# Moving element-wise work between VectorE, GpSimd and ScalarE in a fused RWKV-5 attention and mixture-of-experts kernel, and issuing a gather and a flag earlier

## The chip, the core and the metric

The kernel runs on one core of a Trainium2 chip. The metric is the device time of one execution in microseconds. The kernel before was timed three times (378.99 us median, 377.18 to 380.16), and one more execution of it was profiled.

## The reference, cut to what matters

Attention over 4 batches, 8 heads, 768 tokens, head size 48, with a per-channel decay `w` and a bonus `u`; its output, laid side by side over the heads, is the input `x` (4 x 768 tokens, width 384) of a mixture of 8 experts with one expert per token.

```python
for t in range(S):
    kt, vt, rt = (k[:, :, t], v[:, :, t], r[:, :, t])
    cur = np.einsum('bhd,bhe->bhde', u[None] * kt, vt)
    y[:, :, t] = np.einsum('bhd,bhde->bhe', rt, state + cur)
    state = w[None, :, :, None] * state + np.einsum('bhd,bhe->bhde', kt, vt)
...
fresh_e = int(np.argmax(logits[b, s]))
if s == 0 or local_gate[b, s] < 0.5:
    e = fresh_e
else:
    e = prev_e if prev_e >= 0 else fresh_e
...
h = np.maximum(x[b, s] @ w1[e], 0.0)
out[b, s] = p[e] * (h @ w2[e])
```

The kernel has a fast path for decays inside a band and falls back to a general one where a flag says that some decay lies outside, or that an expert has more tokens than its block.

## The kernel before, in words

**Order.** The program is scheduled by hand (`tc.manual_schedule()`): each engine runs its instructions in the order in which the Python emits them, and semaphores join the engines. So the order of the calls in `Attention.run` and `Experts.run` is the order of every queue.

**Attention.** There are 16 items, n = 4 * batch + pair of heads. An item's 768 tokens lie in 6 chunks of 128, and it needs these steps:
- `load` (L189): three transfers on SP, `rk` (r and k, transposed), `kv` and `vT`, three items ahead; four buffers for rk and vT, five for kv.
- `scale` (L203), on GpSimd, called one item ahead: `ke` = k times the decay to the chunk's end (L213), `pd` = r times k (L217), and from item 3 on `rw` = r times the powers of w (`decayed`, L230). Each is two instructions, called halves below; for rw and pd a half is 128 x 384.
- `keys` (L232), on VectorE: `kw` = k times the inverse powers (L237), which lie in PSUM (`inv`). For items 0 to 2 the same function makes rw on VectorE too, from a copy of the powers in PSUM (`first`, part of the PSUM tile `mp`). `reciprocals(i)` (L153) makes the inverse powers of pair i in two VectorE instructions.
- TensorE: `added` (L249) makes the chunks' sums, VectorE's scan in `states` (L255) turns them into states S, `scores` (L291) multiplies kw by rw in two halves of three chunks, VectorE masks each half into `am` (L293), `own` (L268) makes the bonus term, which VectorE multiplies by v (L276), `inside` (L300) adds am times v and `before` (L313) adds S times rw. ScalarE copies the result out of PSUM (L321), `turn` (L332) transposes it, ScalarE copies that into `x` (L334), and after a batch's last pair ScalarE's queue sends x to memory (L337).

Step n of the loop in `Attention.run` holds, in this order: turn(n-2), added(n), states(n), scale(n+1), inside(n-1), before(n-1), the first half of the scores of item n+1 with its mask, the second half of its scores, own(n), keys(n+2), and the mask of the second half. Step 4 makes up the lead: it calls keys for items 4, 5 and 6 and scores for items 4 and 5. The scores, turn and logits share two PSUM tiles (`pairs`), which `banks` hands out by turns: a call waits until the tile of the call before last has been read.

**Routing.** After a batch's last pair, `logits` (L345) and `token_logits` (L351, L352) give the gate logits. Batches 0 and 1 are routed inside the attention's steps 9 to 15: ranks, slots, two one-hot tables (`columns` L813 and `places` L824 on VectorE, `apart`/`same` on ScalarE), `numbers` (L818, GpSimd), and `summed` (L846, TensorE), which turns them into token numbers per expert; `copied` (L852) and `head` (L856, L860, L876, L877) give the indices `gid0`. Then `gather(0)` (L1107) fetches the first expert's 168 token rows from memory with two indirect DMAs on GpSimd's queue.

**Experts.** `Experts.run` holds ten units: two early experts with 168 slots each, filled from batches 0 and 1, then eight blocks. A unit of the first kind runs, for m = 0 to 7, `hidden` (L1134), `output` of m-1 (L1221), then `routing(8 i + m)`, and for the last m the transposes of the next unit's rows (`turn`, L1120, copied out by L1121). `routing(0)` to `routing(12)` route batches 2 and 3 in the same way as above: `routing(4)` emits the ranks, slots and one-hot tables and, last, `blocks` (L783 to L790), all on VectorE; `routing(7)` has `summed`. Expert 0's weights come as four transfers of 768 KB (`piece(0)` to `piece(3)`, L1096, on SP), each behind a one-element copy on ScalarE; expert 1's come on ScalarE's queue at m = 1. All transposes of this part share two PSUM tiles (`tp`), which `bank` hands out by turns.

**The flag.** `flag(0)` (L1693 to L1696, VectorE) counts the decays inside the band on each partition into `some`; `flag(1)` (L1698, TensorE, then L1699 and L1700 on VectorE) adds the partitions up; `flag(2)` joins it with the other count. Parts 0 and 1 are called in `routing(13)` and `routing(14)`, that is at m = 5 and 6 of unit 1.

## Time and profile before

| | us |
|---|---|
| median of three runs | 378.99 (377.18 to 380.16) |
| the profiled execution, its own time | 379.17 |
| its span in the trace | 377.5 |
| attention: until the first `hidden` starts | 113.0 |
| unit 0, until unit 1's first `hidden` starts | 113.0 to 129.4 |
| unit 1, until block 0's first product | 129.4 to 146.1 |
| the eight blocks | 146.1 to 371 |
| TensorE busy | 363.0 (96%) |
| VectorE, GpSimd, ScalarE busy | 247.7, 148.7, 110.3 |
| granted TensorE clock over the span | 0.996 |

A row of the timeline has the start, the time, the engine and line, the operation, output and inputs, shapes and count, and in brackets the idle time of the engine just before it with what ended that. PE is TensorE's stream of matmuls, PEld its loads of weights, DVE VectorE, ACT ScalarE, POOL GpSimd, SP the queue of transfers. Ends of matmuls are modelled, so PE counts as busy while its pipeline drains; the starts of PEld show best when TensorE went on. 96% busy is an average: in the blocks TensorE has no pause, and what can be won or lost lies in the first 146 us.

### The profile page before, as it was taken

How to read it: one execution, taken by the hardware profiler on the slowest of the kernel's cores; microseconds unless marked ns; L12 is line 12 of the kernel's file. 1: busy time of each engine (PE TensorE's matmuls, PEld its weight loads, DVE VectorE, ACT ScalarE, POOL GpSimd, SP SyncE). 2: the span in 40 equal slices, each digit the busy share in tenths (PEclk: the TensorE clock that was granted, in tenths of full speed). 3: DMA queues.
4: the chain of work that ended last, by engine and by line, in shares of the span. 5: the costliest groups of instructions: out<-in, count | busy, mean ns of one | idle time of the engine just before them, and what ended most of it. 6: DMA issues, size and time to landing. Idle time of an engine off the chain costs nothing. (4 is left out here: it accounts for less than half of the span.)

```text
span 377.5 us, 9676 instructions
## 1 busy us (share of the span) xinstructions
PE 363.0 (96%) x3844; PEld 319.6 (85%) x3844; DVE 247.7 (66%) x718; ACT 110.3 (29%) x304; POOL 148.7 (39%) x207
## 2 busy tenths in 40 slices
PE   7899999999989999999999999999999999999992
PEld 6676777786769998999899999999999998989971
DVE  6988778888834835787557656857767767555300
ACT  4132233233532211322332233333243233331210
POOL 7689999786222055212333113313233023021012
PEclk9999999999999999999999999999999999999998
DMA  7999999983669457713352452164165065162011
GB/s 245 417 411 410 407 405 338 370 300 109 196 232 340 160 188 296 299 27 115 140 198 62 147 214 87 49 218 190 38 207 213 22 215 206 21 257 112 2 41 38
DMA packets 17765, 74.93 MB, mean 199 GB/s; under 512 B 2778, under 2 KB 6624, under 8 KB 15408
## 3 DMA queue, kind: packets, MB, share of 16 engines
q1 hardware_dynamic: 10336, 56.89, 40.7%
q0 software_dynamic: 3424, 9.48, 7.4%
q10 hardware_dynamic: 3952, 7.87, 5.7%
q8 instruction: 32, 0.52, 0.6%
q14 instruction: 21, 0.17, 0.1%
HBM read 64.79 MB, written 9.47 MB: 197 GB/s over the span
## 5 line engine op out<-in xcount | busy, mean ns | idle before, releaser
L1333 POOL DMA_INDIRECT out_dram<-yo,sid x27 | 26.6, 985 | 115.5 <-ACT yo L1328 92.0
L1184 PE MATMUL h<-exT,w1t 128*128 128x168 f32 (+4 forms) x240 | 54.9, 327 | 0.0
L1188 DVE TENSOR_TENSOR hT<-h,hs 128x168 f32<-128x168 f32 (+3 forms) x60 | 21.1, 351 | 46.1 <-PE h L1184 29.6
L1107 POOL DMA_INDIRECT xg<-x_d,gid x29 | 31.1, 1072 | 34.1 <-DVE gid L877 15.1
L1184 PEld LDWEIGHTS h<-exT,w1t 128*128 128x128 f32 x240 | 41.6, 190 | 0.3 <-issue 0.3
L1134 PE MATMUL h<-exT,w1t 128*128 128x168 f32 (+2 forms) x192 | 37.2, 333 | 0.5 <-DVE lt L698 0.5
L1253 PE MATMUL y<-factors,sums 128*128 128x192 f32 x168 | 36.8, 326 | 0.0
L293 DVE TENSOR_TENSOR am<-pair,kept 128x768 f32<-128x768 f32 x32 | 30.0, 953 | 8.9 <-PE pair L291 8.4
L217 POOL TENSOR_TENSOR pd<-rk 128x384 f32<-128x384 f32 x32 | 31.5, 1006 | 10.6 <-PE y L268 10.0
L1184 PE MATMUL h<-xs,ws 128*128 128x168 f32 (+4 forms) x144 | 35.3, 327 | 0.0
L1134 PEld LDWEIGHTS h<-exT,w1t 128*128 128x128 f32 x192 | 30.9, 190 | 2.6 <-DVE lt L698 0.6
L1184 PEld LDWEIGHTS h<-xs,ws 128*128 128x128 f32 x144 | 25.5, 190 | 4.3 <-ACT hs L1191 1.2
L1253 PEld LDWEIGHTS y<-factors,sums 128*128 128x128 f32 x168 | 28.9, 190 | 0.2
L291 PE MATMUL pair<-rw,kw 48*64 48x128 f32 (+1 forms) x768 | 23.4, 249 | 1.9 <-issue 1.1
L300 PE MATMUL y<-am,kv 128*64 128x128 f32 x360 | 22.9, 276 | 1.3 <-DVE y L276 1.2
L230 POOL TENSOR_TENSOR rw<-rk,tab 128x384 f32<-128x384 f32 x26 | 23.7, 936 | 0.4 <-DMA rk<-in_rk_dram 0.4
L1121 DVE COPY exT<-tp 128x384 f32<-128x384 f32 (+5 forms) x29 | 13.9, 485 | 14.7 <-PE tp L1120 14.6
L291 PEld LDWEIGHTS pair<-rw,kw 48*64 48x64 f32 x768 | 19.6, 133 | 4.6 <-issue 2.8
L1253 PE MATMUL y<-w2t,hT 128*128 128x192 f32 x96 | 23.0, 328 | 0.0
L213 POOL TENSOR_TENSOR ke<-kv,endT 128x288 f32<-128x288 f32 (+1 forms) x32 | 21.9, 705 | 1.9 <-DMA kv<-in_kv_dram 1.0
L321 ACT COPY xT<-y 128x768 f32<-128x768 f32 x15 | 12.0, 800 | 33.1 <-PE y L313 31.1
L300 PEld LDWEIGHTS y<-am,kv 128*64 128x64 f32 x360 | 19.4, 137 | 2.4 <-DVE y L276 1.7
(298 smaller groups left out, 736.6 us busy)
## 6 DMA issues: line engine op xcount, KB each, us to landing
w1t<-in_w_dram SPq DMA_DIRECT2D x8, 1536.0 KB, 6.9
w2t<-in_w_dram SPq DMA_DIRECT2D x8, 1536.0 KB
rk<-in_rk_dram SPq DMA_DIRECT2D x15, 768.0 KB, 8.4
kv<-in_kv_dram SPq DMA_DIRECT2D x16, 584.0 KB, 7.1
vT<-in_vT_dram SPq DMA_DIRECT2D x16, 384.0 KB
x_d<-x ACTq DMA_DIRECT2D x4, 1152.0 KB
w1t<-in_w_dram SPq DMA_DIRECT2D x2, 768.0 KB
w2t<-in_w_dram SPq DMA_DIRECT2D x2, 768.0 KB
```

The source lines that it names most:

```text
L213: nc.gpsimd.tensor_mul(t["ke"][:, z], t["k"][:, z], spread(self.endT[:, p, hp], 1, len(range(NCH)[z])))
L217: nc.gpsimd.tensor_mul(t["pd"][:, z], t["rT"][:, z], t["kT"][:, z])
L230: engine.tensor_mul(t["rw"][:, z], t["rT"][:, z], spread(pw, 1, z.stop - z.start))
L291: nc.tensor.matmul(sc[f * DP:(f + 1) * DP, h, i, x:], lhsT=t["kw"][q, c, o * DP:(o + 1) * DP], rhs=t["rw"][q, c, x:], start=True, stop=True)
L293: return lambda: nc.vector.tensor_mul(t["am"][:, g], sc, spread(self.kept[:, g:g + 3], 1, 2))
L300: nc.tensor.matmul(t["y"][h][p * DP:(p + 1) * DP, c2 * P:(c2 + 1) * P], lhsT=t["v"][:, (2 * c + h) * DH:(2 * c + h) * DH + DP], rhs=t["am" ...
L1107: self.nc.gpsimd.indirect_dma_start(out=xg[:n], out_offset=None, in_=self.x_d[:rows], in_offset=bass.IndirectOffsetOnAxis(ap=u["gid"][:n, ...
L1134: nc.tensor.matmul(h[:, :n], lhsT=u["w1"][:, m, kk, :], rhs=u["xT"][:, kk, :], start=(kk == 0), stop=(kk == DK - 1))
L1184: nc.tensor.matmul(out, lhsT=a, rhs=b, start=start and k == 0, stop=stop and k == len(terms) - 1, skip_group_check=True)
L1188: nc.vector.tensor_tensor(out, a, b, op=Alu.add)
L1253: return lambda: nc.tensor.matmul(bank[:, x * half:(x + 1) * half], lhsT=a, rhs=b, start=(j == 0 and x == 0), stop=(j == FK // 2 - 1), ski ...
L1333: self.nc.gpsimd.indirect_dma_start(out=out.rearrange("n (h d) -> (n h) d", h=2) if half else out, out_offset=bass.IndirectOffsetOnAxis(ap ...
```

## The change

It does the following.
- **Start.** `reciprocals(1)` on VectorE becomes `inverse(1)`: three GpSimd instructions of 128 x 128 and a ScalarE copy into PSUM. Three warming transposes go. Item 2's second half of rw goes from VectorE to GpSimd, ahead of pd.
- **Items 3 to 8** (`SHARED`). The second half of rw goes from GpSimd to VectorE, right behind kw, read from the table in SBUF.
- **Items 14 and 15** (`LATE`). kw goes from VectorE to GpSimd, ahead of pd, from a copy (`held`) of the inverse powers that ScalarE makes in step 8.
- **Routing of batches 0 and 1.** `columns` moves ahead of the last mask of step 13, `places` is cut in two (end of step 13, middle of step 14), `same` moves to the start of step 14, `numbers` ahead of pd(15), and `summed` and `copied` to the end of step 14, with added(15) ahead of them. `head` and the two gathers move to the start of step 15. The number tables (`numbering`, `cast`) move from steps 2 and 6 to step 8.
- **Transfers.** kv of item 4 is issued ahead of its rk. `piece(1)` stays at the end of the attention's step 14, `piece(3)` is issued behind the gathers, and waits for their rows by a one-element copy on GpSimd.
- **Last item.** `before(15)` runs chunk by chunk over both heads, as for other items, instead of head by head. `own(15)` is no longer cut by `summed`.
- **First unit.** The transposes of unit 0's rows come right after logits(3), ahead of `token_logits` and of `turn(15)`; the second tile's copy goes to ScalarE. So does one of the four copies for block 0.
- **Flag.** `flag(0)` and `flag(1)` move from `routing(13)` and `routing(14)` to `routing(5)` and `routing(6)`; the matmul of `flag(1)` gets its weights spread over 128 columns.

The diff, cut to its core:

```diff
@@ -51,6 +51,8 @@
+LATE = (B * HP - 2, B * HP - 1)
+SHARED = range(3, 9)
@@ -156,6 +159,14 @@
+    def inverse(self, i):
+        nc, w, inv = self.nc, self.tab[:, i, 0, 1:], self.tab[:, i, 1, 1:]
+        nc.gpsimd.tensor_mul(self.more, w, inv)
+        nc.gpsimd.tensor_scalar(self.more, self.more, -1.0, 2.0, Alu.mult, Alu.add)
+        nc.gpsimd.tensor_mul(self.more, self.more, inv)
+        nc.scalar.copy(self.inv[:, i], self.more)
@@ -190,22 +201,25 @@
+        if n == AHEAD:
+            nc.sync.dma_start(out=kv, in_=self.kv_d[b, hp])
...
-        nc.sync.dma_start(out=kv, in_=self.kv_d[b, hp])
+        if n != AHEAD:
+            nc.sync.dma_start(out=kv, in_=self.kv_d[b, hp])
...
-    def scale(self, n):
+    def scale(self, n, ahead=None):
@@ -217,26 +231,44 @@
         def rw(i):
-            self.decayed(nc.gpsimd, n, slice(i * C2, (i + 1) * C2))
+            if i == 0 or n not in SHARED:
+                self.decayed(nc.gpsimd, n, slice(i * C2, (i + 1) * C2))
+        if n == 2:
+            rw(1)
         for what in (pd, ke) if n < 3 else (ke, rw, pd) if n == 4 else (rw, ke, pd):
+            if n in LATE and what is pd:
+                self.keys(n, nc.gpsimd)
+                if ahead:
+                    ahead()
             for i in range(2):
                 what(i)
...
-        pw = self.first[:, :P] if n < 3 else self.tab[:, t["hp"], 0, :P]
+        pw = self.first[:, :P] if n < 3 and engine is self.nc.vector else self.tab[:, t["hp"], 0, :P]
...
-    def keys(self, n):
+    def keys(self, n, engine=None):
+        if n in LATE and not engine:
+            return
         nc, t = self.nc, self.items[n]
+        engine = engine or nc.vector
         t["kw"] = self.two.tile([P, NCH, P], F32, name="kw")
-        inv = self.inv[:, t["hp"]]
-        for z in (slice(0, NCH),) if n > 2 else (slice(0, C2), slice(C2, NCH)):
-            nc.vector.tensor_mul(t["kw"][:, z], t["kT"][:, z], spread(inv, 1, z.stop - z.start))
-            if n < 3:
+        self.room(n)
+        inv = self.held[:, n - LATE[0]] if n in LATE else self.inv[:, t["hp"]]
+        for z in (slice(0, NCH),) if 2 < n < LATE[0] else (slice(0, C2), slice(C2, NCH)):
+            engine.tensor_mul(t["kw"][:, z], t["kT"][:, z], spread(inv, 1, z.stop - z.start))
+            if n < 2 or n == 2 and z.start == 0:
                 self.decayed(nc.vector, n, z)
+        if n in SHARED:
+            self.decayed(nc.vector, n, slice(C2, NCH))
@@ -307,7 +336,7 @@
-        for c, h in [(c, h) for h in range(2) for c in range(1, NCH)] if last else [(c, h) for c in range(1, NCH) for h in range(2)]:
+        for c, h in [(c, h) for c in range(1, NCH) for h in range(2)]:
@@ -376,9 +405,8 @@
                 self.turn_ends(slice(1, HP))
-                self.warm(3)
+                self.inverse(1)
                 self.added(0)
-                self.reciprocals(1)
@@ -398,12 +426,15 @@
                     self.reciprocals(2)
-                else:
-                    router.numbering()
...
                 self.turn(n - 2, pair("tp"))
+                if n == g + 6:
+                    router.same(0, 1)
+                if n == g + 7:
+                    router.head(self.pairs[0][:, 1, C2 * P:])
+                    heads()
@@ -411,7 +442,7 @@
-                    if n not in (g + 3, g + 5):
+                    if n not in (g + 3, g + 5, g + 7):
...
                         self.states(n)
@@ -425,10 +456,10 @@
+            if n == HP * 2:
+                router.numbering()
             if n + 1 < M:
-                self.scale(n + 1)
-            if n == g + 6:
-                router.numbers(0, self.nc.gpsimd)
+                self.scale(n + 1, (lambda: router.numbers(0, self.nc.gpsimd)) if n == g + 6 else None)
@@ -436,12 +467,12 @@
-            if n == g + 6:
-                router.same(0, 1)
-            if M - 2 <= n < M:
-                fetch(2 * (n - M + 2) + 1)
-            if n == 6:
+            if n == M - 2:
+                fetch(1)
+            if n == HP * 2:
                 router.cast()
+                self.held = self.late.tile([P, len(LATE), P], F32, name="held")
+                self.nc.scalar.copy(self.held, self.inv[:, HP - len(LATE):])
@@ -449,14 +480,9 @@
             if n == g + 7:
-                self.own(n, 0)
-                router.summed(0, 0)
-                self.own(n, 1)
-                router.copied(0)
+                self.own(n)
                 spare = self.py.tile([P, 2, 512], F32, name="y")
                 self.turn(n - 1, [spare[:, 0], spare[:, 1]])
-                router.head(self.pairs[0][:, 1])
-                heads()
@@ -465,6 +491,8 @@
                 self.scores(ahead, 0)()
+                if n == g + 6:
+                    router.places(0, slice(3, 6))
                 keep = self.scores(ahead, 1)
@@ -494,6 +522,8 @@
                     self.keys(n + 2)
+                if n == g + 5:
+                    router.columns(0)
                 if 3 < n and ahead < M:
                     keep()
@@ -501,10 +531,12 @@
             if n == g + 5:
-                router.columns(0)
                 router.apart(0, 1)
+                router.places(0, slice(0, 3))
             if n == g + 6:
-                router.places(0, 0)
+                self.added(n + 1)
+                router.summed(0, 0)
+                router.copied(0)
@@ -1092,7 +1123,10 @@
         src = (self.w2 if w else self.w1)[u["e"]].rearrange("p (m x) -> p m x", m=FK)
-        nc.scalar.copy(t[0:1, z.start, 0:1], self.ident[0:1, 0:1])
+        if k == 3:
+            nc.gpsimd.tensor_copy(t[0:1, z.start, 0:1], u["xg"][-1][0:1, 0:1])
+        else:
+            nc.scalar.copy(t[0:1, z.start, 0:1], self.ident[0:1, 0:1])
@@ -1110,7 +1144,7 @@
-    def turn(self, i, j):
+    def turn(self, i, j, copy=None):
@@ -1118,7 +1152,7 @@
-        nc.vector.tensor_copy(u["xT"][:, :, j * P:j * P + n], tp[:, :, :n])
+        (copy or nc.vector.tensor_copy)(u["xT"][:, :, j * P:j * P + n], tp[:, :, :n])
@@ -1403,10 +1437,13 @@
             r.numbers(1)
-            r.places(1, 0)
-            r.places(1, 1)
+            r.places(1, slice(0, 6))
+            r.places(1, slice(6, 12))
             r.blocks()
+        if s == 5:
+            self.flag(0)
         if s == 6:
+            self.flag(1, bank("fp"))
             self.fetch(EARLY, self.nc.sync, 1)
@@ -1428,10 +1465,6 @@
-        if s == 13:
-            self.flag(0)
-        if s == 14:
-            self.flag(1, bank("fp"))
@@ -1441,10 +1474,10 @@
         yb = [self.yps.tile([P, 512], F32, name=f"y{d}") for d in range(DK)]
         att.logits(B - 1, yb[0])
+        for j in range(len(self.units[0]["rows"])):
+            self.turn(0, j, self.nc.scalar.copy if j else None)
+        att.token_logits(B - 1, yb[0])
         att.turn(B * HP - 1, yb[1:])
-        self.turn(0, 0)
-        att.token_logits(B - 1, yb[0])
-        self.turn(0, 1)
         self.router.powers(0)
@@ -1566,7 +1599,7 @@
-                    self.turn(i + 1, m - (FK - after))
+                    self.turn(i + 1, m - (FK - after), self.nc.scalar.copy if following and m == FK - 3 else None)
@@ -1680,7 +1713,7 @@
-        att.run(router, ex.piece, lambda: ex.gather(0))
+        att.run(router, ex.piece, lambda: (ex.gather(0), ex.piece(3)))
@@ -1695,7 +1728,7 @@
-                nc.tensor.matmul(fp[:1, :1], lhsT=some, rhs=router.ones[:, 0:1], start=True, stop=True)
+                nc.tensor.matmul(fp[:, :1], lhsT=some.to_broadcast([P, P]), rhs=router.ones[:, 0:1], start=True, stop=True)
```

23 lines of the change are left out of this document (12 added, 11 removed).

## The prediction

> **What bounds the kernel now.** The page's slices put TensorE at 96% with the clock at full, so I asked first for the busy time by stretches.
>
> ```profile
> 10.00:20.00 10.00, 8.95 (x191) 7.08 (x191) 9.11 (x17) 1.71 (x3) 7.04 (x9) 1.00 1.02 411
> ...
> 30.00:40.00 10.00, 9.05 (x199) 6.31 (x198) 8.16 (x11) 2.11 (x5) 10.00 (x13) 1.00 1.02 408
> 40.00:50.00 10.00, 9.94 (x245) 8.20 (x244) 7.14 (x28) 3.22 (x11) 9.93 (x12) 1.00 1.03 408
> ...
> 110.00:120.00 10.00, 8.94 (x64) 8.19 (x64) 4.33 (x22) 3.00 (x10) 2.46 (x4) 1.00 0.71 249
> ...
> 140.00:150.00 10.00, 9.31 (x63) 8.64 (x61) 6.12 (x21) 2.24 (x7) 5.51 (x10) 1.00 0.68 253
> ```
>
> Columns: TensorE, weight loads, VectorE, ScalarE, GpSimd, clock, DMA. TensorE has pauses in four places only: the first 40 us, the end of the attention, and one spot near 143. From 40 us on it is full although GpSimd is as full as it was before: GpSimd has run ahead and is not what TensorE waits for. So taking work off GpSimd in items 3 to 8 can win nothing there, and work added to VectorE can only cost. Past 146 us TensorE is full to the end; what it loses earlier is never given back. The rest of the reading is the timeline at these places.
>
> **Start.** VectorE sets the pace of steps 1 and 2:
>
> ```profile
> 8.93 1.56 POOL L213 TENSOR_TENSOR ke<-kv,endT 128x288 f32<-128x288 f32 x2
> ...
> 10.89 1.97 POOL L217 TENSOR_TENSOR pd<-rk 128x384 f32<-128x384 f32 x2 [0.40 <-DMA rk<-in_rk_dram]
> ...
> 12.22 0.30 DVE L156 SCALAR_TENSOR_TENSOR mp<-mp,tab 128x128 f32<-128x128 f32 x1 [0.63 <-PE mp L249]
> ...
> 13.32 0.53 DVE L237 TENSOR_TENSOR kw<-rk,inv 128x384 f32<-128x384 f32 x1
> ...
> 14.70 0.55 DVE L230 TENSOR_TENSOR rw<-rk,mp 128x384 f32<-128x384 f32 x1
> ...
> 15.30 0.54 PEld L291 LDWEIGHTS pair<-rw,kw 48*64 48x64 f32 x24 [0.30 <-DVE rw L230]
> ...
> 18.12 1.53 PE L300 MATMUL y<-am,kv 128*64 128x128 f32 x24 [0.82 <-DVE y L276]
> ```
>
> `inverse(1)` takes two instructions of 0.30 us off VectorE. With the three warming transposes gone as well, added(0) and the scan behind it come some 0.5 us earlier, and kw(1) starts near 12.4 instead of 13.32. The new path must be in time. No row shows a 128 x 128 multiplication on GpSimd; by ke (0.78 us for 288 columns) three of them take 1.0 us, with bounds of 0.7 and 1.6. From 10.49, where ke ends, that gives 11.5, and the ScalarE copy 11.9, so it is hidden behind added(0) and the scan by 0.5 us; at the upper bound it is late by 0.1. pd(1) moves from 10.89 to 11.5 and ends by 13.5, before own(1). In step 2 the half of rw that leaves VectorE frees 0.46 us (the spacing of these instructions); on GpSimd it fits in ahead of pd(2). I carry 0.9 plus what step 2 adds to its masks, **1.1 us won**; bounds 0 (the transfers of items 1 and 2, which the row of 10.89 shows late by 0.40, take its place) and 1.6. kv(4) ahead of rk(4) in SP's queue only swaps two transfers that are used near 27 us. The number tables leave GpSimd near 20 us, where it next waits for a transfer: nothing; in step 8 they lie beside its waits for own.
>
> **Items 3 to 8.** In steps 5 and 6 the mask of the second half of the scores frees the PSUM tile that the next scores need:
>
> ```profile
> L230 POOL TENSOR_TENSOR rw<-rk,tab 128x384 f32<-128x384 f32 x26 | 23.7, 936 | 0.4 <-DMA rk<-in_rk_dram 0.4
> ```
> ```profile
> 34.66 1.82 DVE L293 TENSOR_TENSOR am<-pair,kept 128x768 f32<-128x768 f32 x2 [1.17 <-PE pair L291]
> ...
> 45.43 1.97 POOL L217 TENSOR_TENSOR pd<-rk 128x384 f32<-128x384 f32 x2
> ...
> 46.26 0.94 DVE L237 TENSOR_TENSOR kw<-rk,inv 128x768 f32<-128x768 f32 x1
> ...
> 47.12 0.95 DVE L293 TENSOR_TENSOR am<-pair,kept 128x768 f32<-128x768 f32 x1
> ...
> 48.33 0.14 PEld L291 LDWEIGHTS pair<-rw,kw 48*64 48x64 f32 x2
> ...
> 70.71 1.97 POOL L230 TENSOR_TENSOR rw<-rk,tab 128x384 f32<-128x384 f32 x2
> ...
> 71.81 0.89 DVE L709 SCALAR_TENSOR_TENSOR key<-lt,k 128x12 f32<-128x12 f32 x1
> ...
> 114.25 0.17 DVE L709 SCALAR_TENSOR_TENSOR key<-lt,k 128x12 f32<-128x12 f32 x1
> ```
>
> The mask ends at 48.07, the scores start at 48.33: 0.26 us of cover. The new half costs VectorE 0.47 us by its spacing, but there is more. L709, with both tensors in SBUF, takes 0.17 us when GpSimd rests and 0.89 at 71.81, where it ends at 72.70, just as GpSimd's rw does (72.68): it stood until that instruction was through. kw, am and y all have one operand in PSUM and show no such thing. The new half reads r and the table, both in SBUF. In step 5 pd(7) runs until 47.40, so the half starts near 47.3 instead of 47.2 and ends near 47.8; the mask follows 0.65 us late, and the scores lose 0.65 - 0.26 = 0.4. Step 6 is built alike: 0.4. In step 4 two halves come ahead of am(4), which has 1.17 of cover: 2 x (0.47 + half of a GpSimd instruction of 0.94) = 1.9, so 0.7 lost. Item 3's hides behind added(3), item 6's behind a wait of VectorE at 44. **1.5 us lost** in all; bounds 0.4 (GpSimd never in the way) and 4.2 (a whole instruction lost each time: 1.65 + 1.3 + 1.3).
>
> [...]
>
> **Routing and the end of the attention.**
>
> ```profile
> 94.66 1.98 POOL L217 TENSOR_TENSOR pd<-rk 128x384 f32<-128x384 f32 x2 [2.85 <-PE y L268]
> ```
> ```profile
> 103.84 0.59 PEld L846 LDWEIGHTS mp<-ohq,val 128*32 128x32 f32 x24 [0.60 <-issue]
> ...
> 106.45 1.27 POOL L1107 DMA_INDIRECT xg<-x_d,gid  x1 [7.72 <-DVE ex L919]
> ...
> 106.93 1.20 PE L313 MATMUL pair<-rw,S 48*48 48x128 f32 x20
> ...
> 108.62 0.56 DVE L319 COPY end<-pair 128x384 f32<-128x384 f32 x1 [2.30 <-PE pair L313]
> ...
> 111.34 0.55 PE L1120 MATMUL tp<-ident,xg 128*128 128x128 f32 x3 [0.56 <-DMA xg<-x_d,gid]
> ...
> 113.02 1.98 PE L1134 MATMUL h<-exT,w1t 128*128 128x168 f32 x12 [0.50 <-DVE lt L698]
> ```
>
> kw(14) and kw(15) on GpSimd are four instructions of 0.94, which fit into waits like the 2.85 at 94.66; their scores follow 2 us later. VectorE loses two times 0.94 where it does not set the pace. Behind L313 the end is a chain of short waits: head 1's copy at 108.62, the logits, turn(15), the rows at 111.34, their copies, the first `hidden` at 113.02. With L846 (some 0.8) and the index transpose moved into the full step 14, everything up to own(15) comes 1.0 us later, but L300 then waits only for y(15); L313 chunk by chunk gives both heads near 108.3 instead of 108.6; the logits end at 109.5, and the row transposes fill the wait for their copy. The gathers go out near 102.6; before, the rows were there at most 3.6 us after the issue of 106.45 had ended (107.72), so now by 107.5 and 109, with 0.5 us to spare. Then two transposes 0.6, L351 and turn(15) 1.0, so `hidden` starts at 111.15: 1.85 won. From that comes a loss: `places` (0.95 a table half) now runs in step 13 behind numbers and pd(15) on GpSimd, again with both operands in SBUF, and its second part comes right ahead of `summed`: 0.45. **1.4 us won**, bounds 0.4 and 1.9. piece(3) lands behind the gathers, near 113, and is read by `output` of m = 4, past 120; SP's next transfer is at 129, and GpSimd's next instruction behind the waiting copy at 114.56: no cost.
>
> **The flag.**
>
> ```profile
> 125.24 0.39 PEld L1120 LDWEIGHTS tp<-ident,xg 128*128 128x128 f32 x3
> ...
> 128.35 0.16 DVE L790 CAST order<-orderf 1x8 int32<-1x8 f32 x1
> ...
> 129.43 0.90 PEld L1134 LDWEIGHTS h<-exT,w1t 128*128 128x128 f32 x6
> ```
> ```profile
> 140.90 0.16 DVE L1693 TENSOR_SCALAR ok<-w_t 128x4 f32<-128x4 f32 x1
> ...
> 141.36 0.16 DVE L1696 TENSOR_REDUCE some<-ok 128x1 f32<-128x4 f32 x1
> ...
> 142.63 0.19 PE L1698 MATMUL tp<-r_ones,some 128*1 128x1 f32 x2
> 143.50 0.87 PE L1120 MATMUL tp<-ident,xg 128*128 128x128 f32 x6 [0.69 <-DVE over L1699]
> ```
>
> At its old place it costs TensorE 143.50 - 142.63 = **0.9 us, won**. Its new place is worse. `flag(0)` stands in VectorE's queue behind all of routing(4), whose last instruction is L790, ending at 128.51; its four instructions take 0.62 (140.90 to 141.52), so `some` is there at 129.2. TensorE comes to L1698 behind output of m = 5, where now turn(1, 0) starts: 125.24. It stands until 129.2, and with two weight loads goes on at 129.6. Behind it in TensorE's queue are turn(1, 0), hidden(7), `summed`, turn(1, 1) and unit 1, all without a pause (129.43 follows at once), and for `summed` wait the token numbers, the gathers of block 0 and the rest. **4.4 us lost**; bounds 0.3 (only the matmul) and 4.8.
>
> **The sum.** -1.1 + 1.5 - 1.4 - 0.9 + 4.4 = +2.5 us. On the profiled execution's own 379.17 (span 377.5) that makes **381.7 us**; it stands 0.2 above the median of the three runs, 378.99, which I leave in. A measurement of this kernel can tell about 1% from no change, 3.8 us: 375.2 and 382.8.
>
> **Rivals.**
> - *The flag finds VectorE done* (0.17): the wait at L1698 stays near 0.3. That needs VectorE 3.7 us ahead of where it was, from the point of L790. For it: VectorE rests before routing(4). Against it: that rest ends with TensorE's own counts, one m ahead. 381.7 - 4.1 = 377.6, faster than before.
> [...]
> - *The clock falls in the wait at L1698* (0.10):
>
> ```profile
> 4.46 1.50 PEld L163 LDWEIGHTS pair<-ident 128*128 128x128 f32 x8
> ```
> ```profile
> 370.00:371.00 1.00, 0.04 (x2) 0.00 (x0) 0.42 (x1) 0.00 (x0) 0.21 (x1) 1.00 0.25 91
> ...
> 374.00:375.00 1.00, 0.00 (x0) 0.00 (x0) 0.00 (x0) 0.00 (x0) 0.00 (x0) 0.74 0.07 16
> ```
>
>   After the last matmul (370.04) the granted clock halves within 374 to 375, some 4.5 us later. The wait leaves TensorE idle 3.9 us, just short. If it did fall, 4 us at half rate (the slow transposes of 4.46, 0.19 each, show such a start) cost 2: 383.7. [...]
> - *The moves at the start and the end win nothing*, because transfers are late there: within the bounds above, 383 (0.08).
>
> **Chances.** My forecast has 0.48, its own range 379.8 to 383.6. The whole range, 377.0 to 384.5, takes in the first rival and the second up to its centre. Faster by over 1%: 0.05, only the first rival with every other bound in its favour. Slower by over 1%: 0.33, from the second and third and the upper end of my own. Within 1%: 0.62.
>
> **What would show it.** L1698 behind a TensorE wait of about 4 us on L1696, and no wait at the transposes before block 0; if it waits less than 1 us, the forecast falls. L230 on VectorE in steps 4 to 6 taking 0.5 to 1.4 us, ending with a GpSimd instruction. kw(1) near 12.4; first `hidden` 111 to 112; unit 1's first `hidden` some 20.5 us behind it instead of 16.4.

## The result, and the profile after

The changed kernel takes **386.94 us** (median of 6 runs, 385.63 to 388.67); the kernel before, on the same chip, 378.24 (6 runs, 377.18 to 380.16). The ratio is **1.0229** (95% interval 1.0204 to 1.0254): 2.3% slower. The forecast was 381.7, its range ended at 384.5. The profiled execution took 387.11, with a span of 385.3. Ratios, here and below, are taken without the few executions in a slower state of the chip; medians are of all.

Starts of TensorE's work in both profiled executions, and the stages between them:

| stage | before | after | change | forecast |
|---|---|---|---|---|
| until the first `hidden` | 113.02 | 112.98 | 0.0 | -1.0 |
| unit 0, to unit 1's first `hidden` | 16.55 | 24.06 | +7.5 | +4.4 |
| unit 1, to block 0's first `hidden` | 16.55 | 15.52 | -1.0 | -0.9 |
| block 0's first `hidden` to the end | 231.4 | 232.7 | +1.4 | 0 |
| sum (span) | 377.5 | 385.3 | +7.8 | +2.5 |

The forecast is short by some 5.3 us: about 3.1 in unit 0, 1.0 in the attention and 1.4 in the blocks.

**The flag.** VectorE's and TensorE's timeline of the changed kernel around it (start, length, engine and line, operation; in brackets the idle time ahead of it and what ended it):

```profile
125.07 1.02 PE L1255 MATMUL y<-hT,w2t 128*128 128x168 f32 x6
129.63 0.59 PE L1731 MATMUL tp<-r_ones,some 128*128 128x1 f32 x2 [3.54 <-DVE some L1729]
...
129.63 0.50 PEld L1731 LDWEIGHTS tp<-r_ones,some 128*128 128x128 f32 x2 [3.80 <-DVE some L1729]
...
125.69 1.82 DVE L855 TENSOR_TENSOR ohq<-si,iq_i 128x768 f32<-128x768 int32 x2
...
128.89 0.16 DVE L822 CAST order<-orderf 1x8 int32<-1x8 f32 x1
...
129.42 0.16 DVE L1729 TENSOR_REDUCE some<-ok 128x1 f32<-128x4 f32 x1
```

`flag(0)` (now L1726 to L1729) runs behind the last instruction of `routing(4)` (L822), and TensorE stands at `flag(1)` until 129.63. That is the forecast's wait, 3.5 us in the stream of matmuls and 3.8 in the weight loads; the forecast lost 4.4 us there. What the forecast did not carry stands in the stretches behind it (columns: length, TensorE, weight loads, VectorE, ScalarE, GpSimd, granted clock, DMA share, GB/s):

```profile
126.00:127.00 1.00, 0.09 (x1) 0.00 (x0) 1.00 (x2) 0.00 (x0) 0.00 (x0) 1.00 0.50 209
...
128.00:129.00 1.00, 0.00 (x0) 0.00 (x0) 0.86 (x6) 0.00 (x0) 0.00 (x0) 1.00 0.00 0
129.00:130.00 1.00, 0.37 (x2) 0.37 (x3) 0.51 (x5) 0.00 (x0) 0.00 (x0) 0.54 0.00 0
130.00:131.00 1.00, 1.00 (x6) 1.00 (x6) 0.29 (x2) 0.00 (x0) 0.00 (x0) 0.50 0.00 0
...
135.00:136.00 1.00, 1.00 (x19) 0.60 (x11) 0.00 (x0) 0.17 (x1) 0.00 (x0) 0.55 0.95 406
136.00:137.00 1.00, 1.00 (x9) 0.95 (x8) 0.33 (x2) 0.39 (x2) 0.00 (x0) 1.00 0.92 393
```

A mean of 0.54 means that the clock halved 0.92 us before the end of that stretch, at 129.08; the 0.55 of 135 to 136 puts its rise at 135.9. TensorE works in 6.3 of these 6.8 us (from 129.63 on), so half rate cost it 3.1: the rival "the clock falls", which had a chance of 0.10 and a price of 2.

**Block 0.** TensorE now waits for rows that came in time before. GpSimd's gather and SP's transfer that precede, and the transposes that need the rows, in the changed kernel:

```profile
151.45 1.23 POOL L1141 DMA_INDIRECT xg<-x_d,gid  x1 [0.57 <-issue]
...
151.90 0.33 SPq L1113 DMA_DIRECT2D w1t<-in_w_dram  x1
...
159.43 0.31 PEld L1154 LDWEIGHTS tp<-ident,xg 128*128 128x128 f32 x3 [1.58 <-DMA xg<-x_d,gid]
```

In the kernel before, SP's transfer followed the gather by 1.14 us and not by 0.45, and the transposes (at 151.41) did not wait:

```profile
144.32 1.03 POOL L1107 DMA_INDIRECT xg<-x_d,gid  x1 [0.91 <-issue]
...
145.46 0.33 SPq L1082 DMA_DIRECT2D w1t<-in_w_dram  x1
```

**The attention** comes out even, not because nothing happened. Turn(0) starts at 19.29 instead of 20.42, but turn(6) at 56.56 instead of 55.97. In between, TensorE stops in the middle of runs of weight loads (7 and 39 of `scores`, 9 and 11 of `added`), for nothing that the profile names (the kernel before has one such pause there, 0.40 at 34):

```profile
32.89 0.40 PEld L320 LDWEIGHTS pair<-rw,kw 48*64 48x64 f32 x7
34.03 0.87 PEld L320 LDWEIGHTS pair<-rw,kw 48*64 48x64 f32 x39 [0.75 <-issue]
...
39.73 0.30 PEld L281 LDWEIGHTS mp<-kv,ke 128*48 128x48 f32 x9
40.54 0.35 PEld L281 LDWEIGHTS mp<-kv,ke 128*48 128x48 f32 x11 [0.51 <-issue]
```

In step 13, where GpSimd now makes kw (L267), VectorE's smallest routing instructions take 0.41, 0.52 and 1.04 us (0.17 each before), the mask behind them comes late, and turn(12) waits:

```profile
93.05 1.94 POOL L267 TENSOR_TENSOR kw<-rk,held 128x384 f32<-128x384 f32 x2
...
92.14 0.41 DVE L838 SCALAR_TENSOR_TENSOR si<-r,eb 128x12 int32<-128x12 f32 x1
92.59 0.52 DVE L839 TENSOR_SCALAR si<-si 128x12 int32<-128x12 int32 x1
93.03 1.04 DVE L840 TENSOR_SCALAR si<-si 128x12 int32<-128x12 int32 x1
...
94.98 0.80 PE L361 MATMUL pair<-ident,xT 112*128 112x112 f32 x6 [1.06 <-DVE am L322]
```

And two waits at the end of the attention: the head's index transpose (L887) waits for ScalarE's copies of turn(13), since it writes into the PSUM pair that these still read; and SP issues both halves of w2t at 108.85, though the first, piece(2), had its mark by ScalarE at 103.02, so that the first `output` waits (the row puts it down to ScalarE's hT; e1, e6 and e12 name w2t at the same place, and e17 decides):

```profile
103.02 0.18 ACT L1129 COPY w2t<-ident 1x1 f32<-1x1 f32 x1
103.19 0.33 PE L887 MATMUL pair<-ident,rows 128*128 128x128 f32 x1 [0.79 <-ACT x L363]
...
108.85 0.80 SPq L1130 DMA_DIRECT2D w2t<-in_w_dram  x2
...
115.31 1.09 PE L1255 MATMUL y<-hT,w2t 128*128 128x168 f32 x6 [0.43 <-ACT hT L1171]
```

### The profile page after: what moved, and what is told of

Same layout as the page of the kernel before. It is cut to its first block, busy times and chain, and to the rows that moved or that the text cites. A ratio compares the mean times of both kernels' runs of the same rounds, so it can differ in the third digit from the quotient of the medians.

```text
span 385.3 us, 9677 instructions
## 1 busy us (share of the span) xinstructions
PE 365.5 (95%) x3841; PEld 321.9 (84%) x3841; DVE 250.3 (65%) x718; ACT 111.4 (29%) x307; POOL 150.5 (39%) x210
## 5 line engine op out<-in xcount | busy, mean ns | idle before, releaser
L1218 PE MATMUL h<-exT,w1t 128*128 128x168 f32 (+4 forms) x240 | 54.9, 327 | 0.0
L1218 PEld LDWEIGHTS h<-exT,w1t 128*128 128x128 f32 x240 | 41.6, 190 | 0.3 <-issue 0.3
L1168 PE MATMUL h<-exT,w1t 128*128 128x168 f32 (+2 forms) x192 | 38.0, 338 | 0.0
L1218 PE MATMUL h<-xs,ws 128*128 128x168 f32 (+4 forms) x144 | 35.3, 327 | 0.0
L1168 PEld LDWEIGHTS h<-exT,w1t 128*128 128x128 f32 x192 | 31.7, 195 | 2.0 <-issue 0.2
L1218 PEld LDWEIGHTS h<-xs,ws 128*128 128x128 f32 x144 | 25.5, 190 | 4.3 <-ACT hs L1225 1.2
L329 PEld LDWEIGHTS y<-am,kv 128*64 128x64 f32 x360 | 19.4, 137 | 2.3 <-DVE y L305 1.5
L256 POOL TENSOR_TENSOR rw<-rk,tab 128x384 f32<-128x384 f32 x21 | 19.6, 947 | 1.9 <-DMA rk<-in_rk_dram 1.9
```

The source lines that it names most:

```text
L256: engine.tensor_mul(t["rw"][:, z], t["rT"][:, z], spread(pw, 1, z.stop - z.start))
L329: nc.tensor.matmul(t["y"][h][p * DP:(p + 1) * DP, c2 * P:(c2 + 1) * P], lhsT=t["v"][:, (2 * c + h) * DH:(2 * c + h) * DH + DP], rhs=t["am" ...
L1168: nc.tensor.matmul(h[:, :n], lhsT=u["w1"][:, m, kk, :], rhs=u["xT"][:, kk, :], start=(kk == 0), stop=(kk == DK - 1))
L1218: nc.tensor.matmul(out, lhsT=a, rhs=b, start=start and k == 0, stop=stop and k == len(terms) - 1, skip_group_check=True)
```

## The experiments

Two edits come back in most of them. **Flag early**:

```diff
         if s == 2:
+            self.flag(0)
             r.turn_runs(1, bank("rp1"))
         if s == 3:
+            self.flag(1, bank("fp"))
             r.last(1, bank("bc1"))
...
-        if s == 5:
-            self.flag(0)
         if s == 6:
-            self.flag(1, bank("fp"))
```

**Rows first**:

```diff
-                    self.gather(i + 2, slice(j, j + 1), u[FK - 2 + j // 2])
+                    self.gather(i + 2, slice(j, j + 1), u[FK - 3 + j // 2])
```

The table has TensorE's starts in the profile of each run, and the ratio of its times to those of the kernel before on the same chip (95% interval).

| kernel | turn(0) | turn(6) | turn(11) | first hidden | unit 1 | block 0 | span | ratio |
|---|---|---|---|---|---|---|---|---|
| before | 20.42 | 55.97 | 89.20 | 113.02 | 129.57 | 146.12 | 377.5 | |
| e10 before again | 20.41 | 56.35 | 88.87 | 113.32 | 129.87 | 146.43 | 377.7 | |
| after | 19.29 | 56.56 | 88.64 | 112.98 | 137.04 | 152.56 | 385.3 | 1.0229 (1.0204-1.0254) |
| e1 | 19.31 | 56.36 | 88.47 | 111.92 | 129.53 | 145.23 | 378.2 | 1.0024 (1.0001-1.0046) |
| e2 | 19.41 | 56.68 | 88.75 | 112.20 | 134.03 | 149.55 | 382.2 | 1.0132 (1.0102-1.0162) |
| e3 | 19.41 | 56.42 | 88.50 | 112.84 | 130.21 | 145.73 | 378.4 | 1.0061 (1.0031-1.0090) |
| e4 | 20.00 | 55.35 | 87.38 | 110.59 | 132.64 | 148.16 | 380.8 | 1.0171 (1.0119-1.0223) |
| e15 | 19.32 | 56.38 | 88.78 | 112.83 | 130.50 | 146.02 | 380.1 | 1.0049 (1.0018-1.0081) |
| e5 | 19.43 | 56.73 | 89.16 | 114.12 | 130.81 | 146.34 | 380.4 | 1.0084 (1.0054-1.0114) |
| e6 | 19.32 | 56.61 | 89.11 | 112.67 | 130.46 | 145.98 | 378.7 | 1.0068 (1.0040-1.0095) |
| e9 | 19.37 | 56.37 | 88.86 | 113.75 | 131.21 | 146.74 | 378.0 | 1.0045 (1.0024-1.0067) |
| e14 | 20.00 | 56.40 | 88.39 | 111.69 | 129.19 | 144.72 | 377.4 | 1.0095 (1.0065-1.0125) |
| e12 | 19.41 | 56.55 | 88.93 | 111.91 | 129.67 | 145.20 | 376.5 | 1.0018 (1.0002-1.0035) |
| e18 | 19.40 | 56.81 | 88.91 | 111.88 | 128.57 | 144.10 | 376.6 | 0.9985 (0.9964-1.0007) |
| e11 | 20.05 | 56.00 | 88.23 | 111.26 | 128.13 | 143.66 | 376.0 | 0.9988 (0.9963-1.0014) |
| e16 | 20.49 | 56.43 | 88.68 | 112.01 | 129.47 | 144.99 | 376.3 | 0.9979 (0.9954-1.0004) |
| e17 | 20.01 | 55.95 | 88.23 | 111.56 | 128.25 | 143.77 | 375.1 | 0.9957 (0.9935-0.9979) |

### The flag

**e1: the flag at its old place, all else changed.** `flag(0)` and `flag(1)` go from `s == 5` and `6` back to `13` and `14`.

> The changed kernel with the flag's two parts back at m = 5 and 6 of unit 1; all else as changed. My theory: the new place costs 7.6 us in unit 0 (a wait of some 4.3 at L1731, and 3.3 for half the clock behind it), and the old one 1.0 in unit 1. Unit 0 (first hidden to unit 1's first hidden) should be 16.4 again, unit 1 16.5, and the clock full. If the late rows before block 0's turn come only from unit 1 being 1.0 shorter, that wait of 1.4 goes too and the time is 386.9 - 7.6 + 1.0 - 1.4 = 378.9; if they come from something else in the change, 380.3. Rival: unit 0 is long for another part of the change (the order of the routing): then it stays above 384.

Measured 379.93 (10 runs). Unit 0 takes 17.6 instead of 24.1: the flag's place was the loss. It is not 16.4, since the first `output` now waits 0.9 for w2t. Unit 1 takes 15.7: the stall of 0.9 stayed away although the flag is back (one of the row copies around it is on ScalarE now, which may be why; not tried), and the wait in block 0 stayed.

**e2: TensorE kept busy in the wait.**

```diff
         if s == 6:
-            self.flag(1, bank("fp"))
+            fp = bank("fp")
+            for _ in range(36):
+                self.nc.tensor.transpose(fp[:, :P], self.ident, self.ident)
+            self.flag(1, fp)
```

> The changed kernel with 36 transposes of the identity, some 3.7 us of work nobody reads, ahead of the flag's matmul on TensorE. My theory: the wait on VectorE stays, since the transposes lie inside it, but TensorE is never idle, so the clock stays at 1.0 in 129 to 136 and the 3.3 us of half rate go: 386.9 - 3.3 = 383.6, unit 0 20.7 long. Rival: the clock falls for the load of the chip (transfers at 430 GB/s just ahead of it), not for TensorE's rest: it falls all the same and the time stays at 387.

Measured 384.09 (4 runs). The weight loads, and the stretches around them:

```profile
125.59 3.99 PEld L1448 LDWEIGHTS tp<-ident 128*128 128x128 f32 x36
129.56 0.30 PEld L1734 LDWEIGHTS tp<-r_ones,some 128*128 128x128 f32 x2
```
```profile
125.00:130.00 5.00, 5.00 (x47) 5.00 (x46) 4.11 (x15) 0.31 (x1) 0.00 (x0) 1.00 0.35 144
130.00:135.00 5.00, 5.00 (x56) 4.57 (x55) 1.73 (x6) 0.88 (x3) 0.00 (x0) 1.00 0.56 187
```

The flag's matmul is as late as in the changed kernel, but the clock stays at 1.00, and the ratio is 0.0097 lower (3.7 us; 3.3 expected). In the profile unit 0 is 2.2 shorter, with 0.6 more of waiting at the first `output`, so some 2.8 for the clock, near the 3.1 worked out above. So the half clock comes from TensorE's rest, and is a cost of its own beside the wait.

**e3: flag early.**

> The changed kernel with the flag's VectorE part at m = 2 and its matmul at m = 3 of unit 0, where VectorE rests 3.5 us ahead of L772. My theory: no wait, no half clock, and no stall in unit 1: unit 0 16.4, unit 1 15.5. With the wait before block 0's first turn still there (1.4, since unit 1 is short) 386.9 - 7.6 = 379.3; without it 377.9. Rival: the four instructions delay the chain of the routing at any place of unit 0, and the token numbers come late for it: 380 to 382, with a wait at summed.

Measured 380.53 (9 runs): 6.4 us less than the changed kernel by the ratios. No wait, clock 1.00 from 115 to 140, unit 1 15.5. The 1.2 before block 0's second turn is still there. The rival's wait at `summed` does not appear.

**e4: the flag's move alone, in the kernel before.** `flag(0)` and `flag(1)` at `s == 5` and `6`.

> The kernel before with one part of the change alone, the flag at m = 5 and 6 of unit 0. My theory: the wait and the half clock come from the place alone: +7.6 in unit 0, -1.0 in unit 1, and +1.4 before block 0 if the rows are late because unit 1 is shorter: 378.2 + 8.0 = 386.2, or 384.8 if that wait stays away. Rival: the wait needs the other moves (places cut in two, an earlier start of unit 0): then below 381.

Measured 384.26 (4 runs). Unit 0 takes 22.05 (+5.5), with the same 3.54 of wait, and only half as long at half rate:

```profile
126.65 0.19 PE L1697 MATMUL tp<-r_ones,some 128*1 128x1 f32 x2 [3.54 <-DVE some L1695]
```
```profile
127.00:128.00 1.00, 1.00 (x8) 1.00 (x7) 0.72 (x3) 0.00 (x0) 0.00 (x0) 0.78 0.00 0
128.00:129.00 1.00, 1.00 (x6) 1.00 (x5) 0.00 (x0) 0.27 (x1) 0.00 (x0) 0.50 0.00 0
...
130.00:131.00 1.00, 1.00 (x18) 0.71 (x20) 0.00 (x0) 0.00 (x0) 0.00 (x0) 0.51 0.65 221
131.00:132.00 1.00, 1.00 (x21) 0.75 (x14) 0.22 (x1) 0.27 (x1) 0.00 (x0) 1.00 0.89 381
```

From 127.56 to 130.98, 3.4 us, where the changed kernel had 6.8. TensorE's last matmul had ended at 123.11, so the clock fell 4.5 us behind it, when TensorE had been at work again for 0.9: a wait need not last until the fall to cause it. The move alone makes the kernel 1.7% slower (1.2 to 2.2); the rival falls.

**e15: only the producer early.** `flag(0)` at `s == 2`, `flag(1)` left at `s == 6`.

> The changed kernel with only the flag's VectorE part moved, to m = 2 of unit 0; its matmul stays at m = 6. My theory: the 7.6 us come from where the producer stands in VectorE's queue (behind the 9 us of routing(4)), not from the matmul's place in TensorE's: no wait at L1731, full clock, the same time as with both parts moved, 380.5. Rival: TensorE waits at m = 6 for something else that routing(4) makes (the tile of the bank, which VectorE reads late): a wait of 1 us or more stays, over 382.

```profile
125.14 1.02 PE L1255 MATMUL y<-hT,w2t 128*128 128x168 f32 x6
126.00 0.28 PE L1730 MATMUL tp<-r_ones,some 128*128 128x1 f32 x2
126.14 0.53 PE L1154 MATMUL tp<-ident,xg 128*128 128x128 f32 x3
```

The matmul at its new place costs 0.14 us, with no wait and the clock at 1.00 from 115 to 135. Measured 381.38 (10 runs), ratio 1.0049 against e3's 1.0061: the same. The whole cost lay in where the producer stood in VectorE's queue.

### Block 0's rows

**e9: flag early, rows first.**

> The changed kernel with the flag at m = 2 and 3 of unit 0 (380.5), and the gathers for block 1 released by the hidden product one m earlier in unit 1. My theory: these rows are late because w1t's transfer is issued 0.4 us behind the first gather (144.63 and 145.07), and in the kernel before 1.1 behind it (144.32 and 145.46, a lead that its stall at the flag gave): with a lead of over 1.5 the wait of 1.2 before block 0's second turn goes, and the time is 380.5 - 1.2 = 379.3. Rival: the rows share the way with w2t's transfer, which is under way in either case: the wait stays within 0.3 of 1.2.

```profile
144.77 1.03 POOL L1141 DMA_INDIRECT xg<-x_d,gid  x1 [0.55 <-issue]
...
146.08 0.33 SPq L1113 DMA_DIRECT2D w1t<-in_w_dram  x1
```

The lead is 1.3 us, the wait is gone, and from block 0 to the end it takes 231.3, as in the kernel before. Measured 380.07 (12 runs), ratio 1.0045 against 1.0061; the intervals overlap, so the stage shows it more clearly than the time. Over all runs: with a lead of 0.12 to 0.62 us (after, e1 to e6, e14, e15) the wait was there every time; with 1.14 to 1.46 it was absent in before, e9, e10, e12, e16 and e17, but 1.1 and 1.3 in e11 and e18. The lead decides most of it; what remains in those two is open.

### The attention

**e10: the kernel before once more.**

> The kernel before once more, unchanged, for a second profile. In the kernel with only the flag moved, whose attention is the same code, step 13 came at 87.4 instead of 89.2 and the first hidden product at 110.6 instead of 113.0. My theory: before's first profile had pauses of TensorE (0.84 of issue at 85, 0.4 at 34 and others) that most executions do not have, and the changed kernel's attention is to be compared with 110.6: then this profile has no pause at 85, step 13 near 87.4 to 88 and the first hidden product near 111. Rival: the pauses belong to the kernel before and vanish with any change of the code: 89.2 and 113.0 again.

Measured 379.51, once. The pause of 0.84 at 85 is gone, others came elsewhere: turn(11) 88.87, first hidden 113.32. e4, whose attention has the same instructions, had 110.59. So one execution's attention wanders by 2 us and more, and a difference of that size between the attentions of two single profiles carries no verdict.

**e13: flag early, no transfers for items 5 to 8.** `load(n)` returns ahead of its three transfers for these items; what comes behind the attention (2769 us in all) says nothing.

> The changed kernel with the flag at m = 2 and 3, and without the loads of items 5 to 8 (their attention works on the data of earlier items, so the output is not the reference's): no transfers of theirs between 19 and 38 us. My theory: TensorE's pauses put down to issue at 27.3, 33.9 and 40.4 (0.34, 0.76 and 0.41 us) are waits for its own instructions, which come by a queue of transfers and lie behind the loads: with the DMA engines at rest they are gone, and turn(1) to turn(6), 33.4 in this version, takes 1 to 1.5 less. Rival: the pauses are a dependence that the profile does not name (kw, rw or a mask): they stay, each within 0.15 of its size.

Only its attention is read. The weight loads at the same places as above, and the DMA engines' share there:

```profile
27.20 0.26 PEld L324 LDWEIGHTS pair<-rw,kw 48*64 48x64 f32 x9
28.12 0.87 PEld L324 LDWEIGHTS pair<-rw,kw 48*64 48x64 f32 x39 [0.66 <-issue]
...
33.50 1.13 PEld L324 LDWEIGHTS pair<-rw,kw 48*64 48x64 f32 x46
...
36.22 0.16 PEld L378 LDWEIGHTS pair<-xT,wp 128*32 128x32 f32 x8 [1.15 <-DVE am L326]
...
40.24 0.53 PEld L285 LDWEIGHTS mp<-kv,ke 128*48 128x48 f32 x20
```
```profile
20.00:25.00 5.00, 4.83 (x100) 3.62 (x102) 3.82 (x6) 2.25 (x6) 3.84 (x6) 1.00 1.02 412
25.00:30.00 5.00, 4.53 (x114) 3.37 (x111) 4.14 (x8) 0.83 (x2) 5.00 (x7) 1.00 0.20 75
30.00:35.00 5.00, 4.66 (x122) 4.03 (x124) 5.00 (x7) 1.50 (x3) 5.00 (x7) 1.00 0.02 7
```

The second and third pause are gone (46 and 20 loads in one piece), the first, behind a DMA share of 1.02 until 25 (0.20 from 25 to 30), is not. The trace has a queue of instructions, q8, in packets of 16 KB. In the changed kernel TensorE went on at 27.51, the next of these packets was under way from 31.65 to 32.74, and TensorE stood until 34.03; in e13 it went on at 28.12, the packet came from 29.61 to 30.54, and no pause followed. The packet ahead of e13's first pause was under way from 25.58 to 26.66, at the transfers' end. But turn(1) to turn(6) takes 32.8 instead of 33.4, 0.6 less and not 1 to 1.5: the mask of step 4 takes the pauses' place (1.15 at L378, 0.60 in the kernel before).

**e14: flag early, the start as before.** `inverse(1)` becomes `warm(3)` and, behind added(0), `reciprocals(1)`; item 2's rw all on VectorE; kv(4) behind rk(4).

> The changed kernel with the flag at m = 2 and 3, and the start as it was: pair 1's inverse powers on VectorE behind added(0), three warming transposes, item 2's rw all on VectorE, kv(4) behind rk(4). My theory: the start's 1.1 are real at step 2 (turn(0) back from 19.4 to 20.4), but given back by step 8, since TensorE's pauses at 27 to 40 grow when it comes earlier: step 8 stays within 0.4 of 56.4 and the time within 0.5 of 380.5. Rival: the 1.1 are kept and hidden under another loss: step 8 near 57.4, time 381.5.

Turn(0) at 20.00, turn(6) at 56.40 against e3's 56.42: what the start wins is used up by step 8, as expected. The time does not decide between theory and rival: 381.84 (5 runs), ratio 1.0095 against 1.0061, a difference inside the intervals.

**e5: flag early, nothing shared.** `SHARED = ()`.

> The changed kernel with the flag at m = 2 and 3 of unit 0 (380.5, the base of this comparison), and the second half of items 3 to 8's rw back on GpSimd. My theory: these halves cost the attention some 1.6 us in steps 3 to 8 (they wait on VectorE for the instruction that GpSimd is in): turn of step 4 to turn of step 8 takes 26.6 instead of 27.4, step 13 comes near 87, and the time is 380.5 - 1.6 = 378.9. Rival: what the start won is given back at TensorE's own pauses (the ones put down to issue, 0.3 to 0.6 us at 27, 34 and 40), which do not depend on rw: then step 13 stays at 88.5 and the time at 380.5.

A miss for my theory, and as its rival had it: 381.05 (12 runs), ratio 1.0084, no gain. Step 4 is 0.5 shorter (turn(2) to turn(3) 9.43; 9.7 to 10.4 in every profile with the halves shared, 9.2 to 9.5 in before, e4 and e10), but TensorE's own pauses came later instead, turn(6) at 56.73.

**e6: flag early, kw of items 14 and 15 on VectorE.** `LATE` empty, `numbers` still ahead of pd(15).

> The changed kernel with the flag at m = 2 and 3 of unit 0 (380.5), and kw of items 14 and 15 back on VectorE. My theory: GpSimd's kw holds up VectorE's small routing instructions in step 13 (si: 0.41, 0.52 and 1.04 instead of 0.17 each), and with them the mask for which turn(12) waits 1.06: without it these are 0.17 again, that wait is below 0.4, and the time is 380.5 - 0.8 = 379.7. Rival: VectorE gets two instructions of 0.94 more in steps 12 and 13 and is late by these instead: 380.5 to 382.

```profile
92.90 0.17 DVE L836 SCALAR_TENSOR_TENSOR si<-r,eb 128x12 int32<-128x12 f32 x1
93.11 0.17 DVE L837 TENSOR_SCALAR si<-si 128x12 int32<-128x12 int32 x1
93.19 0.17 DVE L838 TENSOR_SCALAR si<-si 128x12 int32<-128x12 int32 x1
```

The three are back at 0.17, and turn(12) does not wait; turn(11) to turn(12) takes 5.2 instead of 5.3 to 6.9. The time does not follow: 380.71 (12 runs), ratio 1.0068. What comes sooner there is waited for later: in e1 and e12 the first `hidden` starts 1 us before the changed kernel's, and the first `output` then waits 0.9 and 0.8 us for w2t.

### Putting it right

**e12: what is lost outside the flag, undone.** Flag early, rows first, `LATE` empty, and

```diff
-                    router.head(self.pairs[0][:, 1, C2 * P:])
+                    router.head(self.pairs[1][:, 1, C2 * P:])
```

> The changed kernel with the flag at m = 2 and 3 of unit 0, block 1's gathers one m earlier, kw of items 14 and 15 on VectorE, and the head's index transpose in the other PSUM pair, which no copy of turn(13) reads. My theory: of the change's losses outside the flag, 1.4 sit before block 0's second turn, 0.8 in the head's wait for ScalarE, 0.2 to 1.6 in the late mask of step 13; with these three gone the time is 380.5 - 1.4 - 0.8 - 0.7 = 377.6, level with the kernel before (378.2) or a little under it. Rival: the rows of unit 0 come no sooner than the tables allow, the waits move there (behind the row transposes of unit 0), and the time stays at 379 to 380.

Measured 378.61 (12 runs), ratio 1.0018, where 0.998 was expected. The three waits are gone or below 0.4; one of 0.84 for w2t has come.

**e11: the kernel before with flag early and rows first, nothing else.**

> The kernel before with the flag at m = 2 and 3 of unit 0, and block 1's gathers released one m earlier in unit 1; nothing else of the change. My theory: the flag's only cost in the kernel before was the stall of 0.9 in unit 1, and its only use there was the lead that it gave these gathers; with the lead kept by the earlier release the 0.9 are won: unit 1 15.5 to 15.6 instead of 16.5, the blocks 231.3 as before, ratio 0.9975 (378.2 - 0.9 = 377.3). Rival: the earlier gathers get in the way of block 0's rows or of w2t: ratio 1.000 or above.

Measured 377.32 (12 runs), ratio 0.9988: unit 1 is 15.5 as expected, but a wait of 1.1 for block 1's rows stayed, and a gain is not shown.

**e16: only the moves at the end.** As e12, with the start and `SHARED` as in e14 and e5.

> The changed kernel with the flag at m = 2 and 3, block 1's gathers one m earlier, the head's transpose in the other PSUM pair, and with items 3 to 8, items 14 and 15 and the start as in the kernel before: what is left of the change is the routing's order, the earlier gather and the first unit's order. My theory: the attention up to step 13 is then the kernel before's (87.4 to 89.2), and the end of the attention (turn(11) to the first hidden product) 23.0 instead of 23.2 to 24.4: ratio to the kernel before 0.996 to 0.999. Rival: the moves at the end win nothing, ratio 1.000 to 1.003.

Measured 378.09 (12 runs), ratio 0.9979, its interval just reaching 1. Turn(11) to the first hidden takes 23.3, inside what the kernel before's code takes (23.0 to 24.5 in before, e4, e10 and e11): the moves at the end alone win nothing yet. The ratio is where the theory had it, but unit 1, 1.0 shorter for the flag, is enough for it.

**e17 and e18: piece(2) ahead of the gathers,** in e16 and in e12.

```diff
+                if n == M - 1:
+                    fetch(2)
                 if n == g + 7:
                     router.head(self.pairs[1][:, 1, C2 * P:])
                     heads()
-                if n >= M - 2:
-                    fetch(2 * (n - M + 2))
+                if n == M - 2:
+                    fetch(0)
```

> As the kernel with only the moves at the end (flag at m = 2 and 3, block 1's gathers earlier, the head's transpose apart, start and items 3 to 8, 14 and 15 as before; ratio 0.9979), with piece(2) ahead of the gathers in step 15. In the changed kernel piece(2), the half of w2 that the first output reads, stands on SP behind piece(3), which waits for the gathered rows: ready at 103, issued at 108.8. My theory: this is where the end of the attention's win goes (0.4 to 0.9 us of wait at the first output, put down to w2t or to hT): issued near 103 it lands before the first hidden product ends, the wait goes, and the ratio is 0.996 to 0.997. Rival: the gathers then share the way with 768 KB more, the rows land later than 110.2, and the wait only moves to unit 0's row transposes: ratio 0.998 or above.

> The same order of piece(2) and the gathers in the changed kernel with its start and its items 3 to 8 kept (flag at m = 2 and 3, gathers earlier, transpose apart, kw of items 14 and 15 on VectorE; ratio 1.0018). My theory: its wait of 0.84 at the first output for w2t goes: ratio 0.9995. Rival: as above, 1.0015 or more.

```profile
111.56 1.89 PE L1167 MATMUL h<-exT,w1t 128*128 128x168 f32 x12
113.29 1.02 PE L1254 MATMUL y<-hT,w2t 128*128 128x168 f32 x6
...
102.37 6.96 SPq L1129 DMA_DIRECT2D w2t<-in_w_dram  x2
```

In e17 the first half goes out at 102.37 (the last row joins both halves) and the first `output` follows the first `hidden` without a pause. **377.02** (12 runs) against 378.48, ratio **0.9957 (0.9935 to 0.9979)**: 0.4% faster than the kernel before. In e18 the wait is gone too, 378.18, ratio 0.9985 against e12's 1.0018. The intervals overlap those of e16 and e12, so what piece(2) is worth shows in the stage, not in the time.

## Why the prediction was wrong, point by point

- **The flag (+4.4): the mechanism right, a step missing.** The wait came where and for what the forecast said, 3.5 to 3.8 us long. But the forecast took 4.5 us, the time from the last matmul to the fall of the clock at the end of the kernel, for the rest that TensorE may have, and so gave "the clock falls in the wait at L1698" a chance of 0.10 and left its price out of the sum. That comparison is the step that failed: in the changed kernel the clock fell 3.0 us after TensorE's last matmul and cost 3.1; in e4 it fell 4.5 us after it, as in the prediction's row, though TensorE had rested only 3.5 and was at work again. e2 separates the clock from the wait: 3.7 us by the ratios, some 2.8 in the stage. The 4.5 us rested on one row; what sets the moment of the fall no run shows. The mean clock is at most 0.990 in five of the six executions of the changed kernel and 0.993 to 0.997 in nearly all of the kernel before, so 0.10 was far too low; the price was 3.1 us here and 1.7 in e4, against 2 in the forecast.
- **The old place (-0.9): right where it was looked for, given back elsewhere.** Unit 1 is 1.0 shorter. The stall had also given block 1's gathers a lead over w1t's transfer (1.14 us before, 0.45 after); without it 1.4 comes back as a wait in block 0. The prediction asked what the stall costs, not who used it. e9 shows it in the stage.
- **Start (-1.1): right at step 2, not at step 8.** Turn(0) starts at 19.3 to 19.4 in ten profiles with the new start (19.87 in e13) and at 20.0 to 20.5 in seven with the old one, so 0.6 to 1.2 are won there. The lower bound, 0, was the right one in the end, though for another reason than late transfers of items 1 and 2. From 27 to 41, with the DMA share at 1.02, TensorE pauses behind the packets of q8, and with the new start it pauses longer (1.91 us in three pauses of the weight loads in the changed kernel, 1.51 in three in e3; with the old start one of 0.40 in before, one of 0.47 in e14); and in step 4 the masks are late. e13 removes two pauses and finds the mask next (e14, e3: the same turn(6)). The prediction looked for TensorE's pauses after 40 us by averages over 10 us and so missed this kind, of which the profile before has one of 0.84 at 85.
- **Items 3 to 8 (+1.5): too much.** The halves on VectorE take 0.54 to 1.10 us, as forecast from 0.5 to 1.4, with GpSimd in the way: of the six in the changed kernel the four of 0.70 to 1.10 end 0.41 or 0.42 us behind the end of a GpSimd instruction that was under way when they began (26.12, 32.30, 47.70 and 53.27). In step 4 that is some 0.5 on the path (0.7 forecast), in steps 5 and 6 nothing is seen of the 0.4 each: e13 and e14 pass step 5 in 5.85, the kernel before at best in 5.87. Taking the halves back won nothing (e5).
- **Routing and the end (-1.4): none of it arrived.** Three waits stand in its place: kw on GpSimd in front of VectorE's routing (0 to 1.6 at turn(12); the prediction looked only at GpSimd's own waits for room, though it had reckoned with VectorE's waits for GpSimd in items 3 to 8), the head's transpose in a tile that is still read (0.8), and w2t (0 to 1.0), whose piece(2) stands on SP behind piece(3), which waits for the gathered rows. The prediction followed piece(3) to where it is read and not to what stands behind it in SP's queue. With these mended and the flag early, e17 is faster than the kernel before.
- **The rivals.** Their chances were 0.17, 0.17, 0.10 and 0.08. The first, "the flag finds VectorE done", and the second, "whole GpSimd instructions lost" (each new half on VectorE behind a whole one: 4.2 instead of 1.5, 384.4), did not happen; the fourth, "nothing won at the start and the end", did, beside the third, the clock.

## What to carry to other kernels

A small instruction whose result another engine waits for belongs in its engine's queue ahead of the long block, however cheap it is: the producer's place cost 7 us, the consumer's 0.14. A wait of TensorE of 3.5 us cost twice here, once for itself and once for half rate behind it (1.7 or 3.1 us); behind a wait of 2.5 us in block 0 of e15 two weight loads of L1218 took 0.33 to 0.38 us (at 154.99, 155.32 and 158.19), as ahead of it (0.38 at 150.55 and 150.93), so no half rate shows. And before taking out a stall, ask which transfer or instruction used that time; before delaying a transfer, read what is behind it in its queue.

## What the runs showed of the hardware

- **The length of the wait does not settle alone when the clock falls, nor for how long.** The same wait of 3.54 us was followed by 6.8 us at half rate in the changed kernel and by 3.4 in e4. The clock fell 3.0 and 4.5 us after the last matmul. In the changed kernel TensorE had rested 3.0 us when it fell and began again 0.55 us later; half rate lasted from 129.08 to 135.9. In e4 TensorE had begun again 0.9 us ahead of the fall, and half rate lasted from 127.56 to 130.98 (one profile each). What sets the moments of the fall and of the rise these runs do not show.
- **TensorE's unnamed pauses follow the packets of an instruction queue.** The pauses inside one run of loads vanished where the transfers were left out (e13, two of three). The profile lists an instruction queue, q8, of 32 packets, 0.52 MB, beside the data queues, and these pauses follow it: in 17 of the 18 profiles there are 42 of them of 0.35 us or more between 27 and 86 us, and each ends 1.2 to 1.6 us after a packet of this queue has landed. From one pause to the next TensorE runs 252 or 253 instructions (252 and 253 in the changed kernel from 27.51 to 34.03 and to 40.54; below, matmuls and weight loads of e3, second and third column):

```profile
27.32:33.86 6.54, 5.63 (x126) 4.41 (x127) 6.09 (x9) 1.44 (x3) 6.54 (x9) 1.00 1.02 410
33.86:40.41 6.55, 5.72 (x126) 3.46 (x127) 5.95 (x7) 1.14 (x4) 6.55 (x8) 1.00 1.03 415
```

That q8 is TensorE's queue, and that TensorE waits there for its own instructions, is inferred from these numbers; the profile does not name the queue's engine. With the DMA share at 1.02, from 27 to 41 us, a pause was 0.34 to 0.76 us long in the changed kernel and in e3.
